# A new order of steps for a tightly scheduled attention-and-experts kernel: constants first, weights for the output last, fewer dummy matmuls

## The chip, the core and the metric

The kernel runs on one core of a Trainium2 chip. The metric is the device time of one execution in microseconds (us). Several executions were taken of each kernel, and each experiment was timed in the same rounds as the kernel before, on the same chip. A run is called slow when it lies over 1.5% above the fastest of its kernel; comparisons below use the other, fast runs.

Five engines work side by side, each through its own instruction stream in order: TensorE (PE in the profile's lines; its weight loads are PEld) multiplies matrices, ScalarE (ACT) computes functions, VectorE (DVE) and GpSimd (POOL) do elementwise work, SyncE (SP) starts transfers; 16 DMA engines move data. TensorE's *granted clock* is the share of its full speed that the profile's clock records show.

## The reference, cut to what matters

```python
mag = np.sqrt(a_re*a_re + a_im*a_im)             # (4, 8, 768, 48): batch, head, time, channel
scale = np.minimum(mag, 0.999) / (mag + 1e-06)   # the complex decay, its size capped
for t in range(768):                             # linear attention with a decaying complex state
    S_re, S_im = ar*S_re - ai*S_im + k[t] (x) v[t], ar*S_im + ai*S_re
    y[t] = q[t] @ S_re
x = y as (3072 tokens, 384)
out = (sigmoid(x @ w_gate) * (x @ w_val)) @ w_out    # 384 -> 1536 -> 384
```

## The kernel before

Time is cut into 6 chunks of 128 steps; with 4 sequences this makes 24 *slabs* of 128 tokens and 384 channels. Slabs are handled in nine *groups* of 1, 1, 2, 4, 4, 4, 4, 2 and 2. Within a chunk the decays become logarithms and phases, which are summed along time by fp32 matmuls; the last phase of a chunk is carried to the next chunk by a small transfer (a *hop*). Each slab then has scores, a state and an output `y`, which is transposed and goes through the gate and value matmuls of its group.

All of it is a list of named steps. Each has a number in `TIMES`; sorting by these numbers gives the order in which the steps are written to the in-order instruction streams of the engines. They are no times of the chip.

```python
SIZES = [1, 1, 2, 4, 4, 4, 4, 2, 2]
# decays of slab m, group g
add(("sq", m), ...)    # ScalarE: squares of a_re, a_im        (after the loads lr, la of slab m)
add(("add", m), ...)   # GpSimd: sum of the squares
add(("min", ...), ...) # GpSimd: cap, once per two slabs
add(("lna", g), ...)   # ScalarE: log of a group        } these need one table of functions,
add(("lnm", g), ...)   # ScalarE: log of the sizes      } tanh, sin and arctan need others:
add(("inv", g), ...)   # ScalarE: exp(-log)             } each switch is one ACT_TABLE_LOAD
add(("r", ...), ...)   # GpSimd: ratio                  -> ("atan", g) on ScalarE
add(("cl", m), ...)    # TensorE: cumulative sums, fp32 -> ("ee", m) exponentials on ScalarE
add(("hop", m), ...)   # GpSimd queue: carry of the phase -> ("ct", m), ("nid", m) TensorE
# ... sines "cs", products "qke", "ks", "qs", transposes "tp", scores "sc", "y", "xp", "xt" ...
t_moe = kind("moe", 4, [L, 512], F32, psum)   # four PSUM buffers for gate, value and output
for fb in range(NFB):                         # 12 blocks of the hidden layer
    add(("pg", g, fb), ...)     # TensorE: gate
    add(("pv", g, fb), ...)     # TensorE: value
    add(("tanh", g, fb), ...)   # ScalarE: tanh of the gate
    add(("p", g, fb), ...)      # VectorE: (tanh + 1) * value
# "po": output matmuls with wo; "ot": scaling; "st": store
...
order = plan.order(TIMES)                     # sorted by TIMES; adds a "table" step at each switch
for key in order:
    if key[0] == "table":
        nc.scalar.preload_act_table_set(SETS[key[1]])
        continue
    st = plan.steps[key]
    for n in st[2]:
        tiles[n] = plan.bufs[n](n)
    for _ in range(WARM.get(key, 0)):         # dummy matmuls ahead of this step
        nc.tensor.matmul(warm_of(tiles[st[2][0]]), zero, zero, start=True, stop=True)
    st[0](tiles)
```

Of the kernel before, what the change touches and what calls it, by code (L numbers as in the profile page):

```python
# [34 lines left out]
        3.57, 5.49],  # L35
    "wg": [
        28.263, 7.549, 23.318],
    "wv": [
        30.844, 31.664, 9.765],
    "wo": [  # L40
        37.677, 33.061, 38.497],
    "lr": [
        0.04, 0.45, 14.208, 19.927, 12.031, 27.419, 43.37, 24.787, 53.034,
        71.13, 63.694, 61.674, 77.312, 83.312, 79.472, 77.722, 107.913,
        110.073, 108.733, 111.993, 150.47, 185.542, 182.86, 184.072],
    "la": [
        0.86, 2.2, 20.947, 18.967, 22.867, 32.518, 40.682, 17.017, 57.834,
        71.91, 62.634, 56.874, 80.432, 88.622, 82.352, 78.228, 108.323,
        122.256, 131.294, 111.033, 150.88, 171.936, 186.502, 189.892],
    "sq": [  # L50
        4.73, 5.69, 24.437, 25.174, 28.029, 41.292, 50.764, 30.44, 66.726,
        77.988, 76.988, 72.777, 92.103, 104.991, 99.025, 83.273, 114.177,
        127.024, 135.003, 116.725, 175.031, 194.324, 190.832, 198.199],
    "add": [
        5.599, 6.595, 25.342, 26.296, 33.881, 42.197, 51.669, 34.835, 68.555,
        82.855, 77.893, 73.682, 96.999, 116.036, 107.784, 97.953, 115.082,
        145.007, 141.883, 131.112, 175.936, 195.229, 197.196, 208.669],
    "min": [
        6.179, 11.162, 27.361, 43.728, 53.776, 84.92, 79.325, 118.143,
        119.046, 146.538, 151.278, 196.293, 210.891],  # L60
    "lna": [
        6.427, 7.678, 26.042, 55.473, 88.108, 123.53, 158.229, 196.725,
        221.563],
    "lnm": [
        6.844, 12.805, 28.766, 56.85, 86.731, 122.153, 161.353, 197.462, 222.3],
    "inv": [
        7.261, 8.226, 26.91, 58.226, 89.616, 125.647, 159.976, 198.936,
        223.037],
    "r": [
        7.81, 8.811, 29.083, 63.293, 59.771, 92.922, 91.161, 129.351, 127.59,  # L70
        161.521, 163.281, 199.841, 223.942],
    "cl": [
        8.081, 15.614, 32.195, 34.117, 61.599, 58.377, 59.726, 67.931, 88.259,
        90.329, 95.326, 96.524, 127.983, 123.871, 124.517, 133.416, 167.245,
        166.376, 168.741, 170.993, 199.291, 198.645, 224.126, 229.088],
    "ee": [
        12.065, 19.814, 34.502, 35.242, 62.446, 59.603, 60.573, 68.914,
        91.363, 92.84, 98.285, 97.545, 128.83, 124.907, 127.761, 134.263,
        168.221, 168.961, 169.701, 171.84, 203.738, 199.673, 228.465, 229.935],
    "scr": [  # L80
        12.621, 23.277, 35.716, 41.092, 63.414, 70.44, 70.16, 69.47, 98.381,
        99.121, 98.841, 98.101, 129.386, 135.509, 129.666, 134.819, 171.376,
        171.096, 171.656, 172.756, 204.599, 200.852, 230.771, 230.491],
    "rbe": [
        17.607, 28.029, 65.514, 72.93, 100.311, 138.175, 177.434, 207.039,
        238.046],
    "lk": [
        3.16, 8.421, 6.04, 23.827, 16.057, 52.074, 50.154, 48.796, 84.272,
        76.068, 90.542, 53.994, 105.359, 114.303, 81.392, 151.29, 125.658,
        118.047, 160.423, 170.316, 183.27, 163.02, 194.892, 205.289],  # L90
    "lq": [
        5.08, 18.167, 28.827, 35.306, 58.794, 54.954, 60.714, 55.914, 87.662,
        85.232, 91.502, 70.72, 105.769, 114.713, 89.582, 156.48, 141.003,
        142.753, 162.083, 172.346, 188.932, 196.432, 205.699, 207.999],
    "lv": [
        4.12, 21.907, 29.83, 37.994, 51.114, 46.108, 64.554, 86.702, 118.457,
        69.75, 117.637, 126.068, 59.754, 146.608, 102.279, 135.099, 141.953,
        140.593, 121.846, 164.56, 204.879, 197.392, 148.087, 193.932],
    "v16": [
        10.585, 32.484, 43.151, 53.2, 54.679, 52.623, 71.27, 94.682, 122.562,  # L100
        117.567, 120.407, 133.338, 138.97, 149.378, 116.991, 145.962, 147.441,
        176.984, 141.307, 202.387, 211.793, 225.703, 168.944, 242.96],
    "qke": [
        13.699, 21.557, 35.916, 44.631, 69.509, 61.532, 65.054, 80.228,
        99.487, 108.739, 106.023, 101.248, 136.629, 125.829, 139.546, 159.59,
        171.644, 169.883, 182.979, 186.798, 204.66, 206.908, 229.387, 231.148],
    "atan": [
        9.937, 10.354, 32.471, 65.128, 94.874, 131.234, 165.181, 201.707,
        225.777],
    "ct": [  # L110
        11.182, 12.386, 34.763, 33.359, 69.276, 70.241, 71.049, 76.463,
        98.778, 102.372, 105.608, 107.064, 139.369, 142.805, 149.621, 146.87,
        169.853, 175.014, 177.614, 176.458, 205.553, 209.07, 229.734, 230.58],
    "r16": [
        14.565, 13.233, 35.61, 36.076, 70.123, 71.088, 74.604, 78.859,
        100.788, 103.906, 106.95, 108.481, 144.071, 144.537, 150.814, 151.28,
        171.66, 176.295, 184.888, 185.354, 206.4, 209.947, 230.581, 231.513],
    "nid": [
        16.26, 13.833, 36.838, 36.676, 70.887, 71.695, 75.254, 80.175,
        101.388, 106.254, 110.099, 113.499, 145.393, 147.516, 152.21, 163.64,  # L120
        172.26, 177.104, 186.677, 186.84, 208.184, 214.896, 231.226, 232.912],
    "cr": [
        17.78, 18.15, 39.747, 44.566, 72.407, 75.461, 90.993, 80.539, 106.204,
        110.192, 129.57, 116.355, 149.48, 159.606, 154.383, 166.557, 175.768,
        180.232, 195.061, 193.954],
    "cs": [
        16.623, 14.516, 37.276, 38.433, 71.25, 74.041, 75.831, 81.172,
        101.751, 109.035, 110.562, 117.938, 147.194, 151.592, 152.749,
        164.024, 173.874, 177.467, 187.184, 189.675, 208.548, 215.574,
        231.969, 233.276],  # L130
    "ks": [
        17.912, 23.392, 38.565, 47.386, 72.539, 75.33, 77.395, 86.683, 103.04,
        110.9, 111.851, 120.334, 148.483, 155.763, 154.209, 166.393, 175.163,
        179.327, 189.969, 193.181, 214.402, 219.049, 233.258, 235.59],
    "qs": [
        18.778, 24.258, 39.431, 48.651, 73.405, 76.196, 80.124, 89.08,
        104.372, 114.182, 113.316, 124.671, 149.349, 158.152, 156.629,
        168.045, 177.995, 181.003, 191.434, 197.045, 215.867, 219.915,
        234.124, 240.153],
    "tp": [  # L140
        19.778, 20.425, 28.256, 25.258, 41.58, 40.431, 51.31, 54.189, 74.808,
        79.728, 84.774, 77.843, 89.882, 87.183, 92.675, 93.122, 119.088,
        109.005, 125.163, 122.777, 115.604, 118.641, 130.376, 132.746,
        159.946, 156.257],
    "qkT": [
        20.426, 21.073, 29.326, 25.905, 45.924, 41.229, 55.436, 54.837,
        78.261, 81.759, 85.421, 84.658, 90.95, 87.882, 93.408, 94.606,
        119.735, 117.003, 125.811, 123.424, 116.405, 122.28, 131.425, 133.555,
        160.594, 161.193],
    "sc": [  # L150
        24.476, 28.033, 35.967, 26.638, 54.636, 43.128, 56.168, 62.971,
        85.659, 87.957, 93.569, 94.865, 95.972, 94.642, 98.437, 98.158,
        129.502, 131.872, 129.279, 126.26, 135.335, 133.192, 136.208, 134.462,
        162.766, 162.543, 163.802, 167.022, 169.387, 169.61, 173.973, 172.932,
        192.406, 187.002, 193.924, 199.937, 201.683, 200.16, 204.457, 204.68,
        224.972, 231.389, 233.075, 233.298, 242.63, 239.009, 246.424, 245.801],
    "mst": [
        27.662, 28.727, 36.542, 27.062, 56.034, 49.517, 56.634, 63.614,
        86.084, 88.48, 94.007, 95.804, 96.403, 95.205, 99.256, 98.657,
        130.769, 132.49, 129.703, 127.009, 135.951, 134.154, 136.632, 134.886,  # L160
        163.567, 162.967, 164.632, 167.446, 169.874, 170.473, 174.504,
        173.638, 194.647, 188.077, 198.062, 200.361, 202.108, 200.96, 205.723,
        205.124, 226.29, 231.979, 236.456, 234.99, 243.251, 241.685, 246.934,
        246.335],
    "kv": [
        20.225, 37.726, 44.375, 59.023, 97.17, 94.442, 99.424, 127.133,
        136.431, 140.015, 138.361, 168.541, 172.039, 161.693, 172.732,
        194.797, 202.557, 206.599, 224.772, 230.38],
    "P": [
        28.261, 40.763, 44.776, 63.148, 97.571, 97.003, 99.856, 127.608,  # L170
        137.232, 143.605, 139.779, 168.942, 172.706, 164.166, 173.172,
        195.246, 202.958, 207.332, 225.173, 231.047],
    "y": [
# [875 lines left out]
```

## Time and profile before

| | before |
|---|---|
| time, median of 3 runs | 286.42 us (286.03 to 288.17) |
| profiled run | 284.33 us, span 282.5 us |
| useful TensorE work, from the spacing of matmul starts | 218 us |
| dummy matmuls / table loads | 534 / 31 |

The page's chain of waits, by engine, shows what the span is made of when one follows back what released what:

```profile
PE 35%; ACT 22%; DMA 13%; POOL 9%; SPq 8%; issue 7%; DVE 4%; ACTq 0%; POOLq 0%; DVEq 0%
```

Only 35% of the way back runs over TensorE (PE), 22% over ScalarE (ACT). A line of a timeline gives start, length, engine, source line, what it did (in brackets: idle time before, and what ended it). The first two are ScalarE's timeline (start, length, engine, source line, what it did): the table load ahead of the logarithms of the first group of four slabs, and the first of these logarithms.

```profile
61.35 1.28 ACT L1012 ACT_TABLE_LOAD   x1
62.65 1.49 ACT L626 ACTIVATE a<-a 128x1536 f32<-128x1536 f32 x1
```

These two are the table by stretches (stretch, length, then busy time and number of instructions of PE, weight loads, VectorE, ScalarE and GpSimd, then granted clock, DMA share, GB/s):

```profile
60.00:90.00 30.00, 28.11 (x341) 22.23 (x339) 17.58 (x35) 26.20 (x47) 20.93 (x19) 1.00 0.81 144
160.00:190.00 30.00, 28.16 (x260) 17.15 (x259) 25.97 (x44) 25.72 (x41) 18.68 (x20) 1.00 0.78 150
```

In the first, TensorE looks busy, but 164 of its matmuls are dummies: by starts, useful work is 17.3 of 30 us, and ScalarE, GpSimd and TensorE take turns. In the second TensorE loses 1.8 us. One of its waits there, from TensorE's timeline (in brackets: idle time before, and what ended it):

```profile
180.78 0.88 PE L741 MATMUL ct<-a,c_t 128*128 128x384 f32 x2 [1.11 <-ACT ee L661]
```

### The profile page before, as it was taken

The numbers are of one execution on the slowest core, as the hardware profiler recorded it, in microseconds if no ns is written. First come the engines' busy times: TensorE is split into PE (matmuls) and PEld (weight loads), VectorE is DVE, ScalarE is ACT, GpSimd is POOL, SyncE is SP. The second block draws the span as 40 slices with busy tenths as digits, with TensorE's granted clock in tenths as the row PEclk, the third lists the DMA queues.
The fourth block names the chain that finished last, engine by engine and source line by source line (L and its number), as shares of the span: only waits on it lengthen the run. The fifth ranks groups of instructions, "written<-read, shape, count | busy, mean of one in ns | idle before, by whom it ended". The sixth has DMA issues, their size and how long they took to land.

```text
span 282.5 us, 6759 instructions
## 1 busy us (share of the span) xinstructions
PE 260.3 (92%) x2586; PEld 179.7 (64%) x2586; DVE 197.2 (70%) x364; ACT 200.3 (71%) x340; POOL 158.4 (56%) x170
## 2 busy tenths in 40 slices
PE   8956994999998999999999999799999999998995
PEld 8735783888767766545774456454457545577784
DVE  3155553672478989898795897798788686697553
ACT  3993992478998997789953999674899559924240
POOL 0604981445968889947999717945449704803000
PEclk9999997799999999999999999999999999999999
DMA  7999999889489944596347769858997744074001
GB/s 146 200 180 194 167 200 195 170 177 207 60 116 201 208 97 57 100 212 139 83 91 121 157 134 210 143 90 129 222 218 105 127 102 102 9 150 107 30 30 56
DMA packets 175344, 38.46 MB, mean 136 GB/s; under 512 B 167992, under 2 KB 175312, under 8 KB 175312
## 3 DMA queue, kind: packets, MB, share of 16 engines
q1 hardware_dynamic: 170688, 34.46, 64.2%
q0 software_dynamic: 4624, 3.57, 8.6%
q8 instruction: 20, 0.33, 0.5%
q14 instruction: 12, 0.10, 0.1%
HBM read 31.01 MB, written 4.76 MB: 127 GB/s over the span
## 4 chain that ended last, share of the span: by engine, by line
PE 35%; ACT 22%; DMA 13%; POOL 9%; SPq 8%; issue 7%; DVE 4%; ACTq 0%; POOLq 0%; DVEq 0%
PE o L984 8%; PE g L948 8%; DMA a<-in_a_im_dram 8%; PE v L948 8%; SPq L579 6%; ACT L1012 5%; ACT sq L605 3%; PE ct L741 2%; PE cl L652 2%; ACT g L958 2%; ACT lm L632 2%; POOL lm L611 2%; DMA qkT<-qst 2%; POOL qk L714 2%; ACT cr L764 2%
## 5 line engine op out<-in xcount | busy, mean ns | idle before, releaser
L958 ACT ACTIVATE g<-g 128x512 f16<-128x512 f32 (+2 forms) x108 | 47.2, 455 | 48.8 <-PE g L948 40.8
L964 DVE SCALAR_TENSOR_TENSOR p<-g,v 128x512 f16<-128x512 f16 (+2 forms) x108 | 52.4, 506 | 32.0 <-PE v L948 15.3
L948 PE MATMUL v<-xt,wv 128*128 128x512 f16 (+2 forms) x324 | 60.9, 313 | 4.6 <-ACT g L958 4.2
L948 PE MATMUL g<-xt,wg 128*128 128x512 f16 (+2 forms) x324 | 59.9, 311 | 1.0 <-ACT g L958 0.5
L984 PE MATMUL o<-wo,p 128*128 128x384 f16 (+1 forms) x300 | 55.5, 319 | 0.0
L714 POOL TENSOR_TENSOR qk<-qk,ee 128x768 f32<-128x768 f32 x23 | 44.7, 1976 | 18.7 <-DMA qk<-in_q_dram 10.9
L611 POOL TENSOR_TENSOR lm<-sq 128x384 f32<-128x384 f32 x23 | 25.4, 1119 | 36.5 <-ACT sq L605 36.3
L948 PEld LDWEIGHTS <-wv 128*128 128x128 f16 x324 | 29.9, 100 | 22.5 <-issue 5.4
L948 PEld LDWEIGHTS <-wg 128*128 128x128 f16 x324 | 30.2, 99 | 21.6 <-issue 4.0
L1012 ACT ACT_TABLE_LOAD x31 | 39.8, 1283 | 0.5
L1018 PEld LDWEIGHTS <-zero 128*128 128x128 f16 x534 | 34.1, 102 | 5.6 <-issue 3.5
L851 DVE TENSOR_TENSOR mst<-sc,c_t 128x512 f16<-128x512 f32 x48 | 32.1, 684 | 6.6 <-PE sc L843 6.4
L984 PEld LDWEIGHTS <-p 128*128 128x128 f16 x300 | 27.0, 97 | 14.1 <-issue 0.9
L643 POOL TENSOR_TENSOR a<-a 128x768 f32<-128x768 f32 (+1 forms) x12 | 20.8, 1746 | 20.3 <-ACT a L637 15.4
L605 ACT ACTIVATE sq<-a 128x768 f32<-128x768 f32 x24 | 20.1, 841 | 14.0 <-DMA a<-in_a_im_dram 13.3
L786 DVE TENSOR_TENSOR kst<-qk,cs 128x768 f16<-128x768 f32 x24 | 23.5, 978 | 9.2 <-ACT cs L778 3.8
L786 DVE TENSOR_TENSOR qst<-qk,cs 128x768 f16<-128x768 f32 x24 | 23.4, 980 | 0.0
L741 PE MATMUL ct<-a,c_t 128*128 128x384 f32 x48 | 20.5, 512 | 1.8 <-ACT ee L661 1.1
L652 PE MATMUL cl<-lm,c_t 128*128 128x384 f32 x48 | 20.4, 514 | 0.8 <-DMA c_t<-glk_c 0.4
L831 DVE COPY qkT<-tp 128x1024 f16<-128x1024 f16 x26 | 17.5, 685 | 3.1 <-PE tp L825 3.0
L733 POOL DMA_DIRECT2D a<-cr x20 | 17.6, 1006 | 2.6 <-ACT a L721 2.2
L747 DVE TENSOR_SCALAR r<-ct 128x384 f16<-128x384 f32 x24 | 12.9, 551 | 8.1 <-PE ct L741 8.0
(64 smaller groups left out, 429.3 us busy)
## 6 DMA issues: line engine op xcount, KB each, us to landing
a<-in_a_re_dram SPq DMA_DIRECT2D x24, 192.0 KB
a<-in_a_im_dram SPq DMA_DIRECT2D x24, 192.0 KB
qk<-in_k_dram SPq DMA_DIRECT2D x24, 192.0 KB
v<-in_v_dram SPq DMA_DIRECT2D x24, 192.0 KB
qk<-in_q_dram SPq DMA_DIRECT2D x24, 192.0 KB
out_dram<-ot SPq DMA_DIRECT2D x23, 192.0 KB
wg<-in_moe_w_gate_dram POOLq DMA_DIRECT2D x3, 384.0 KB, 6.1
wv<-in_moe_w_val_dram POOLq DMA_DIRECT2D x3, 384.0 KB, 7.8
```

What stands on the lines that cost most here:

```text
L605: nc.scalar.activation(out=T[SQ], in_=T[A][:, :, s], func=FT.Square)
L611: eng(g).tensor_tensor(out=T[LM][:, s], in0=T[SQ][:, 0], in1=T[SQ][:, 1], op=ALU.add)
L714: eng(g).tensor_tensor(out=T[QK], in0=T[QK], in1=T[EE], op=ALU.mult)
L741: nc.tensor.matmul(T[CT][:, :HD], wt_t, T[A][:, 1, s], start=True, stop=False, skip_group_check=True)
L786: nc.vector.tensor_tensor(out=T[SL][i].rearrange("p h (r x) -> p h r x", r=2)[:, :, :, 0:D], in0=heads(T[QK][:, i]).unsqueeze(2) .broadcas ...
L851: nc.vector.tensor_tensor(out=T[MS], in0=T[SC], in1=msk_t.unsqueeze(1).broadcast_to([L, 4, L]), op=ALU.mult)
L948: nc.tensor.matmul(T[ACC][:, :nt], w[:, j, fb * 128:fb * 128 + 128], T[XT][:, j, :nt], start=(j == 0), stop=(j == 2))
L958: nc.scalar.activation(out=T[G16][:, :nt], in_=T[PG][:, :nt], func=FT.Tanh, scale=0.5)
L964: nc.vector.scalar_tensor_tensor(out=T[PT][:, fb, :nt], in0=T[G16][:, :nt], scalar=1.0, op0=ALU.add, in1=T[PV][:, :nt], op1=ALU.mult)
L984: nc.tensor.matmul(T[PO][:, :wd], T[PT][:, fb, s * L:(s + 1) * L], wo16[:, fb, c0:c0 + wd], start=(fb == 0), stop=(fb == NFB - 1))
L1012: nc.scalar.preload_act_table_set(SETS[key[1]])
L1018: nc.tensor.matmul(warm_of(tiles[st[2][0]]), zero, zero, start=True, stop=True)
```

## The change

The author gives every step a new number: constants first, gates with less in front of them, fewer GpSimd steps right behind a carry transfer. Buffer slots and dummies (340 in place of 534) follow from the order. No arithmetic changes; five table loads fall away. The core of the diff:

```diff
     "consts": [
-        3.57, 5.49],
+        0, 9.751],
     "wv": [
-        30.844, 31.664, 9.765],
+        10.876, 36.405, 32.691],
     "wo": [
-        37.677, 33.061, 38.497],
+        42.756, 50.985, 47.732],
     "la": [
-        0.86, 2.2, 20.947, 18.967, 22.867, 32.518, 40.682, 17.017, 57.834,
+        0.82, 3.581, 15.146, 15.897, 18.807, 23.826, 24.786, 29.721, 42.831,
     "lna": [
-        6.427, 7.678, 26.042, 55.473, 88.108, 123.53, 158.229, 196.725,
-        221.563],
+        6.019, 10.78, 25.196, 52.172, 85.365, 98.55, 131.983, 162.343, 194.776],
 ... (all other rows of TIMES, SLOTS with the buffer of each tile)
 WARM = {
-    ... 534 dummies, most in the first 45 us
+    ('cl', 0): 2,
+    ('kv', 0): 12,
+    ... 340 in all
```

## The prediction

> **What bounds the kernel now.** I read the page's engine line first, then a table of three stretches (stages), then the chain of waits and the timeline in the stretch with least TensorE work, then the groups.
>
> ```profile
> PE 260.3 (92%) x2586; PEld 179.7 (64%) x2586; DVE 197.2 (70%) x364; ACT 200.3 (71%) x340; POOL 158.4 (56%) x170
> PEclk9999997799999999999999999999999999999999
> DMA  7999999889489944596347769858997744074001
> ...
> L1012 ACT ACT_TABLE_LOAD x31 | 39.8, 1283 | 0.5
> ```
> ```profile
> 0.00:60.00 60.00, 47.29 (x626) 40.90 (x627) 28.09 (x65) 38.34 (x70) 26.86 (x33) 0.94 1.05 182
> 60.00:120.00 60.00, 57.35 (x636) 41.95 (x634) 44.01 (x82) 52.22 (x87) 47.69 (x46) 1.00 0.73 133
> 120.00:283.00 163.00, 155.69 (x1330) 96.81 (x1328) 125.11 (x218) 109.79 (x184) 83.90 (x92) 1.00 0.61 120
> ```
> The columns of the second fence are stretch, length, busy time of PE, its weight loads, VectorE, ScalarE, GpSimd, granted clock, DMA share, GB/s. TensorE's 92% is not all useful: overlapping matmuls count in full, and dummies into `zero` count as work. So I made a ledger from the spacing of matmul starts: a 128x384 matmul of the output takes 0.163 us (four in 0.65 us in the chain), a 512-wide one 0.215, an fp32 pair (cumulative sums) 0.70, a transpose or score 0.056. Times their counts: output 47, gate and value 93, fp32 34, transposes, scores and the small rest 45: **218.5 us useful of a span of 282.5**. The other 64 us are 534 dummies (about 0.06 us each, 32 us) and standing still. By stretch of the trace, useful work is 22 of the first 60 us, 45 of the next 60, 152 of the last 163. So from 120 us on TensorE is the bound, with 11 us lost in 163; before 60 us the bound is the DMA queues (share 1.05, that is, full).
>
> The chain of waits and the timeline of ScalarE show where the first stretch breaks:
> ```profile
> 32.03 0.58 SPq L579
> 32.65 14.51 DMA a<-in_a_im_dram
> 47.23 0.84 ACT sq L605
> ```
> ```profile
> 47.23 0.84 ACT L605 ACTIVATE sq<-a 128x768 f32<-128x768 f32 x1 [4.48 <-DMA a<-in_a_im_dram]
> ```
> One decay load, issued at 32.65, lands 14.5 us later; ScalarE is in order, its square stands ahead of slab 0's gate tanhs, and all engines stand for 4.5 us. The clock records then show half clock from 46.3 to 53.1 us. Near the end there is one more such stop:
> ```profile
> 260.02 0.38 PE L843 MATMUL sc<-qkT,qkT 128*128 128x128 f16 x4 [0.98 <-DMA qkT<-qst]
> ```
>
> **What the skill says.** (1) Perfetto Trace Analysis, "Identifying the Most-Contended Engine": matmul busy share is a poor measure of TensorE's headroom. Agrees: 260 us busy hold 218.5 useful. (2) DMA: Bandwidth & Descriptors, "Queues, rings and completion order": each DMA engine alternates between queues packet by packet. The trace fits: GpSimd's queue (weights) has 4,624 packets of mean 84 ns, SyncE's queue 170,688 of 17 ns, so while weights flow the other loads get little; between 38 and 42 us SyncE's queue moved under 30 GB/s. (3) ScalarE: Activation LUTs, "What ACT_TABLE_LOAD costs": about 1283 ns for any set; the trace has 1283. (4) TensorE: Matmul & The Clock Gate, "Part 1": an idle TensorE falls to half clock and needs some 3.4 us of work to return. The 0.5 records from 46.3 us agree.
>
> **The change, part by part.** No arithmetic changes. Counting the built order of both kernels: DVE, GpSimd, SyncE and real TensorE instructions are equal in number; 194 dummies and 5 table loads go; the rest is order and buffer slots.
>
> *A, the head.* A 192 KB load costs about 1.03 us of all DMA engines (196.6 KB at some 190 GB/s, windows above); a weight piece 2.7 us (4,624 x 84 ns / 16 engines / 9 pieces). Before: the load that stops everything has 25 loads (itself included), 1.3 us of constants and seven weight pieces ahead: 25.8 + 1.3 + 18.9 = 46, plus the start at 1.9: 47.9; seen 47.2. After: that load is issued much earlier, with all but one (slab 7's) of the first eight slabs' squares ahead of the first tanh; the three `wo` pieces move behind the gate. The gate becomes the last value piece, with 27 loads, constants and six pieces ahead: 27.8 + 1.3 + 16.2 + 1.9 = 47.2. So the gate comes no more than 1 us sooner than the 48.3 at which TensorE resumed. But the useful TensorE work standing ahead of the first block that needs it is 11.7 us, against 10.3 at the stop before. Lead: 1.1 + 1.4 = **2.5 us**. Nearly all later TensorE work is one dense stream, so most of a lead in the head lives to the end, unless lost below.
>
> *B, dummies.* 194 x 0.058 = 11 us of TensorE, but they stand where it would wait anyway; they keep the clock. I credit 0. In the first 20 us the old kernel has a nearly unbroken run of them, the new one 2 ahead of the first matmul, so early fp32 pairs run at half clock (some 0.7 us more each, about four of them serial). The head is DMA-bound there, so I charge only 0.3 us.
>
> *C, table loads.* 5 x 1.283 = 6.4 us of ScalarE. The chain has 5.4% = 15.3 us of the 39.8 us of loads on it, so 38%: 2.5 us if they were average ones. Four of the 31 were in the last groups' chain, where TensorE had other work. I credit **1 us**.
>
> *D, the tail.* In program order, useful TensorE work left after the last slab's phase correction (`nid`) is 31.3 us before and 44.2 after. The last slab's transposes have 13 us more cover, so the 0.98 us stop above goes, and some of the small stops in 220-260 us. I credit **1 us**.
>
> *E, GpSimd behind carries.* A carry transfer occupies GpSimd 1.0 us (20 of them, 17.6 us) and what runs behind it is stretched (a 1.81 us product took 2.62 at 145.6 us). The new order still has such runs (three hops and a product, twice or more); GpSimd is 56% busy. Credit 0.3 us.
>
> *F, new gate.* The middle `wo` piece is now issued last, three GpSimd steps after the previous piece, shortly ahead of its output matmuls, which stand in TensorE's order with 21 us useful ahead. If it lands late TensorE stops there. Charge 0.5 us.
>
> Sum: 2.5 + 1 + 1 + 0.3 - 0.3 - 0.5 = **4.0 us**, all from the 64 lost: 286.4 - 4.0 = **282.4 us** (-1.4%). The keys that order the steps are themselves times, and their last store falls from 265.3 to 262.4; I take no time from them, they only say the author hoped for some 1%.
>
> **Rivals.** *R1, the head only swaps its stop.* The first 50 us carry the same kind of bytes; the stop for the decay load becomes one for the value piece or the `wo` piece, with a half-clock spell after it. For: 1.05 DMA share in this stretch. Against: weights of the output move behind the gate. It makes 285-287. *R2, the lead is real but is given back between 60 and 120 us,* where ScalarE is busy 52 of 60 us and GpSimd 48, and the chain runs through them: the group of four slabs must pass logs, sums, phases. For: chain entries of tables, squares, logs at 61-107 us. Against: its squares and logs now stand ahead of the gate. It makes 284-286. *R3, cold clock.* Fewer dummies let TensorE fall to half clock again in 20-60 us; useful 22 us would stretch by up to 10, partly hidden. Against: from 60 to 120 us, with 45 of 60 us useful and few dummies, the records show full clock. 285-289. *R4, ScalarE gain counts in full* (6.4 us instead of 1, with the tail): 279-280.
>
> **Range and chances.** The parts are each uncertain by 1 to 1.5 us; together some 2.5. 8 in 10: **279.2 to 287.0**. Faster by over 2% needs under 280.7, or 5.7 us of the 64: R4 must hold in part, 0.25. Slower needs 292.1, which only a bad R3 gives: 0.04. Same: 0.71.
>
> **What will show it.** A: no 14 us decay load in the chain; TensorE's useful work up to 60 us rises from 22 to 24-25; DMA share stays full to about 50 us; a wait of gate or value matmuls on the value weights at 44-49 us. B: granted clock low in the first 20 us, without delay to the first tanh. C: 26 loads, ScalarE busy near 194 us; the chain's share of them under 5.4%. D: no wait on `qst` after 250 us. F: a wait of the first output matmuls on `wo`, under 2 us. The prediction is wrong if the stretch from 120 us loses much more or less than 11 us (it should lose 8 to 11), or if the half-clock spell grows beyond 7 us after 20 us.

## The result, and the profile after

The kernel after took **275.72 us** (median of 4 runs, 274.39 to 277.63), against 287.3 us for the kernel before in the same rounds. Ratios are the mean time of one kernel's fast runs over that of the other's in the same rounds, so not quite the ratio of these medians: 0.9616, 95% interval 0.9531 to 0.9701. It is faster by 3.8%. The predicted range began at 279.2, and the class that I gave 0.71 (within 2%) was wrong.

How large is the gain really? On the first chip the kernel before had four runs, all over 286 us. In later rounds on other chips it had 7 to 27 fast runs each, with means of 283.1 to 284.4 us, and a tail of runs up to 293. The kernel after had fast means of 275.86, 276.23 and 276.50 us on three chips. The last two ratios are 0.9753 and 0.9716, so the gain between fast runs is some 2.5 to 2.8%, or 7.6 us both times, and the profiled pair says 7.2 us of span. I use "some 7.5 us" from here. My prediction took 4.0 us off a starting time that was itself some 3 us above the kernel's usual fast runs; both add to the miss.

The page of the kernel after: the engine line, the two rows of slices, the chain by engine, and the row of table loads.

```profile
PE 250.8 (91%) x2392; PEld 170.8 (62%) x2392; DVE 199.3 (72%) x364; ACT 193.7 (70%) x335; POOL 166.4 (60%) x170
...
PEclk9995689999999999999999999999999999999999
DMA  8999999998598964599706996499984339581001
...
PE 63%; DMA 10%; ACT 8%; POOL 8%; DVE 6%; issue 3%; SPq 1%; POOLq 0%; ACTq 0%; DVEq 0%
...
L998 ACT ACT_TABLE_LOAD x26 | 33.4, 1283 | 0.5
```

Now 63% of the chain is TensorE, and ScalarE's share went from 22% to 8%. Where was the time earned? I counted the useful TensorE work that each trace had started by a given time (real matmuls only, each at its nominal spacing):

| by (us) | before (us of work) | after | lead |
|---|---|---|---|
| 50 | 12.8 | 14.6 | +1.8 |
| 60 | 20.2 | 20.4 | +0.2 |
| 90 | 37.5 | 42.6 | **+5.1** |
| 120 | 65.0 | 69.1 | +4.1 |
| 160 | 104.7 | 108.3 | +3.6 |
| 190 | 132.2 | 138.2 | **+6.0** |
| 250 | 190.5 | 196.1 | +5.6 |
| 260 | 198.9 | 206.1 | +7.2 |

A *lead* is the useful work that the kernel after is ahead. So at 60 us, after the whole head that the prediction had worked out, there is no lead. It is earned in three places: 60 to 90 us, 160 to 190 us, and a little near 255 us. The lines that answer to those of before, ScalarE's timeline first:

```profile
55.17 1.28 ACT L998 ACT_TABLE_LOAD   x1
56.46 1.48 ACT L612 ACTIVATE a<-a 128x1536 f32<-128x1536 f32 x1
```
```profile
60.00:90.00 30.00, 28.76 (x299) 21.37 (x298) 23.12 (x42) 26.66 (x51) 24.33 (x22) 1.00 0.83 150
160.00:190.00 30.00, 30.00 (x263) 18.00 (x262) 25.21 (x45) 20.49 (x37) 22.02 (x24) 1.00 0.82 144
```

The logarithms of the first group of four start **6.2 us sooner** (62.65 to 56.46), and what hangs on them follows: the arctangent 72.4 to 64.4, the first carry 74.1 to 66.2. The carry gained 8.0 us, more than the logarithms: from the first logarithm to it 11.5 us pass before and 9.7 after. GpSimd has two ratio steps (`a<-a`) on the way, and before, another product stood between them. GpSimd's timeline, before and after:

```profile
68.73 1.81 POOL L714 TENSOR_TENSOR qk<-qk,ee 128x768 f32<-128x768 f32 x1
70.50 1.82 POOL L643 TENSOR_TENSOR a<-a 128x768 f32<-128x768 f32 x1
...
74.14 1.68 POOL L733 DMA_DIRECT2D a<-cr  x2
```
```profile
60.77 3.59 POOL L629 TENSOR_TENSOR a<-a 128x768 f32<-128x768 f32 x2 [5.78 <-ACT a L623]
64.33 1.82 POOL L700 TENSOR_TENSOR qk<-qk,ee 128x768 f32<-128x768 f32 x1
66.18 1.68 POOL L719 DMA_DIRECT2D a<-cr  x2
```

So 6.2 us of the carry's 8.0 are earlier logarithms, and 1.8 us are the order of GpSimd's steps. The traces of the experiments below keep these two lengths: 11.5 us in `y_sq5late`, which has the old order there, and 9.7 us in `s_new84` and `d_stop`, which have the new one.

From 160 to 190 us TensorE is no longer idle at all, and ScalarE is busy 5.2 us less (25.72 to 20.49). Before, it had in this stretch the logarithms of the group with slab 16 (4.4 us, at 167.5 to 172.4) and four table loads (166.2, 172.4, 176.8, 183.7). After, these logarithms stand at 138.2 to 142.8 us, and three table loads are left (164.8, 167.6, 175.9).

### The profile page after: what moved, and what is told of

It reads as the page before. It is cut to its first block, busy times and chain, and to the rows that moved or that the text cites.

```text
span 275.3 us, 6378 instructions
## 1 busy us (share of the span) xinstructions
PE 250.8 (91%) x2392; PEld 170.8 (62%) x2392; DVE 199.3 (72%) x364; ACT 193.7 (70%) x335; POOL 166.4 (60%) x170
## 3 DMA queue, kind: packets, MB, share of 16 engines
q1 hardware_dynamic: 170688, 34.46, 66.2%
## 4 chain that ended last, share of the span: by engine, by line
PE 63%; DMA 10%; ACT 8%; POOL 8%; DVE 6%; issue 3%; SPq 1%; POOLq 0%; ACTq 0%; DVEq 0%
PE g L934 15%; PE v L934 15%; PE o L970 9%; PE cl L638 6%; PE ct L727 5%; DMA a<-in_a_re_dram 2%; PE sc L829 2%; POOL qk L700 2%; POOL lm L597 2%; ACT L998 2%; DMA rbe<-scr 2%; PE cl L1004 1%; DVE mst L837 1%; DMA out_dram<-ot 1%; DMA a<-in_a_im_dram 1%
## 5 line engine op out<-in xcount | busy, mean ns | idle before, releaser
L944 ACT ACTIVATE g<-g 128x512 f16<-128x512 f32 (+2 forms) x108 | 46.7, 457 | 49.1 <-PE g L934 39.9
L700 POOL TENSOR_TENSOR qk<-qk,ee 128x768 f32<-128x768 f32 x23 | 45.8, 2072 | 7.9 <-ACT ee L647 7.6
L934 PEld LDWEIGHTS <-wv 128*128 128x128 f16 x324 | 29.1, 98 | 19.2 <-issue 2.8
L934 PEld LDWEIGHTS <-wg 128*128 128x128 f16 x324 | 29.0, 97 | 18.9 <-issue 2.9
L998 ACT ACT_TABLE_LOAD x26 | 33.4, 1283 | 0.5
L638 PE MATMUL cl<-lm,c_t 128*128 128x384 f32 x48 | 21.8, 545 | 10.2 <-ACT lm L618 10.2
L629 POOL TENSOR_TENSOR a<-a 128x768 f32<-128x768 f32 (+1 forms) x12 | 21.8, 1827 | 10.7 <-ACT a L623 10.6
L772 DVE TENSOR_TENSOR kst<-qk,cs 128x768 f16<-128x768 f32 x24 | 25.2, 1054 | 3.3 <-ACT cs L764 2.5
L1004 PEld LDWEIGHTS <-zero 128*128 128x128 f16 x340 | 23.1, 106 | 5.8 <-issue 3.7
L727 PE MATMUL ct<-a,c_t 128*128 128x384 f32 x48 | 21.2, 528 | 1.6 <-DMA a<-cr 1.1
L693 POOL TENSOR_SCALAR v<-v 128x384 f16<-128x384 f32 x24 | 14.6, 608 | 8.9 <-DMA v<-in_v_dram 7.1
L719 POOL DMA_DIRECT2D a<-cr x20 | 18.7, 1063 | 1.0 <-ACT a L707 0.9
```

The costliest lines, as they stand in the source:

```text
L638: nc.tensor.matmul(T[CL][:, :HD], wl_t, T[LM][:, s], start=True, stop=True)
L700: eng(g).tensor_tensor(out=T[QK], in0=T[QK], in1=T[EE], op=ALU.mult)
L727: nc.tensor.matmul(T[CT][:, :HD], wt_t, T[A][:, 1, s], start=True, stop=False, skip_group_check=True)
L772: nc.vector.tensor_tensor(out=T[SL][i].rearrange("p h (r x) -> p h r x", r=2)[:, :, :, 0:D], in0=heads(T[QK][:, i]).unsqueeze(2) .broadcas ...
L934: nc.tensor.matmul(T[ACC][:, :nt], w[:, j, fb * 128:fb * 128 + 128], T[XT][:, j, :nt], start=(j == 0), stop=(j == 2))
L944: nc.scalar.activation(out=T[G16][:, :nt], in_=T[PG][:, :nt], func=FT.Tanh, scale=0.5)
```

## The experiments

My theory: the path that sets the time is a loop through engines that are each in order, and ScalarE's steps lie on it in two stretches. (1) The stop of ScalarE at 42.75 to 47.2 us before pushed the logarithms, which stand behind the gate tanhs in its stream, and with them everything up to 90 us. (2) Between 160 and 190 us ScalarE's work, table loads among it, lies on that loop and counts in full. The rivals are: more TensorE work standing ready in the head (my part A), the tail (parts C, D), the dummies (part B), or the assignment of buffers. "Fast mean" below is the mean of fast runs; the kernel after is 276.2 us, the kernel before 283.1 to 284.4.

### Buffers or order?

Slots were given out anew in both orders, always the slot that had been free longest (`SLOTS` only; the order of the steps and `WARM` untouched).

> Control: the changed kernel's order with the buffer slots handed out anew, always the one freed longest ago, as the spliced kernels must have it. Both theories (gain from the order of steps / gain from the slots): if the order alone makes the gain, the ratio to before stays near 0.96 (275 to 277 us); if the given slots matter, it falls back by over 1% (279 or more).

> Control: the order of before with slots handed out by the same rule. Order theory: ratio 0.995 to 1.005. Slot theory: off by over 1%.

Measured: new order 276.68 us (fast mean; ratio 0.9821), old order 284.88 (1.0064) where the kernel before had 283.46. With slots by the same rule and on the same chip the two orders differ by 8.2 us, so the order makes the gain. What the given slots add is small but not well measured: 1.4 us in the old order; in the new one 0.5 us by the means, which are from different chips, and 2 to 3 us by the ratios (0.9821 against 0.9753 and 0.9716). The slots given out anew also allowed mixed orders, whose slots must be given out anew.

### Mixed orders

```diff
-order = sorted(steps, key=old number)
+order = [steps whose new number < 55, in new order] + [all others, in old order]   # s_newhead55
+order = [steps whose new number < 84.4 ...]                                        # s_new84
+order = [steps whose new number < 140 ...]                                         # s_new140
+order = [steps whose old number < 192, in old order] + [others, in new order]      # s_old192
 # WARM goes with its step; slots given out anew
```

> Splice: the new order (and its dummies) for every step planned before 55, the old order for all that follow. Theory H (the gain is made in the head and shows at 60 to 90 us, where the decay chain of the first group of four starts some 6 us sooner): 4 to 5 us of the 7 to 11 us are here, ratio 0.980 to 0.986. Theory L (the gain is made in the later order, the head only swaps its stop): ratio 0.995 or more.

> The new order for every step that is planned before 84 us, the old order after it. Ledger theory (4 to 5 us of the gain are earned between 60 and 90 us, in the decay chain of the first group of four slabs): this kernel has some 4 to 5 us of lead at 90 us and keeps it: 280 to 281 us, the rest of the gain (2 to 3 us near 180 and 255 us) stays missing. Rival (the gain is in the tail, by fewer table loads and a longer cover for the last slab): no gain here, 284 to 286 us.

> The new order for all steps planned before 140 us, the old order after. Ledger theory: the lead of 3.5 to 4 us at 140 us is kept, and the 2 to 3.5 us earned near 180 and 255 us are missing: 278 to 279.5 us. Theory that the whole gain comes before 140 us: 276 to 277 us. A new stop at the seam would show as a single wait of several us in TensorE's timeline, and then the run tells nothing of the tail.

> The old order for every step planned before 192 us, the new order for the last 75 us. Ledger theory: only the 1 to 2 us of the last stretch, 283 to 285 us. Rival (gain in the tail): 279 to 281 us.

Measured, as fast means: **283.05** (head to 55 alone, 0.9993), **279.62** (to 84.4, 0.982), 281.23 (to 140, 0.9845), 289.56 (0.9 of the old order, then the new tail, 1.0169).

The head alone earns nothing, which my theory had not expected (0.980 to 0.986). In its trace the logarithms did start early (56.1 us), but behind them GpSimd stood for 6.3 us ahead of slab 5's values, which the old order had put in front of the ratio, and the first carry came at 73.6 us (before: 74.1):

```profile
63.75 0.51 POOL L622 TENSOR_SCALAR v<-v 128x384 f16<-128x384 f32 x1 [6.26 <-PE sc L758]
```

(Its profiled run was slow, so this says what stood in line, not how much it cost.) With the stretch to 84 us added, the lead of the ledger is 4.0 us at 90 us, 1 to 2 from 120 to 250 and 3.3 at the end. So this part of the gain belongs to head *and* first group together. Theory (1), which put it down to ScalarE's stop alone, is too simple: the logarithms come early, and then GpSimd's order must let them through. The last two missed what I expected (278 to 279.5 and 283 to 285 us) and tell little: each has a new stop at its seam. For the new tail this is TensorE's timeline, which loses 5.5 us that neither pure order loses:

```profile
209.00 0.50 PE L899 MATMUL o<-wo,p 128*128 128x384 f16 x1 [5.47 <-DVE p L879]
```

The kernel with new order to 140 us lost 2.0 us of its lead against the kernel after between 170 and 190 us, as `s_new84` did (2.2) and the kernel before did (2.4); then another 3.4 us between 190 and 230 us, where the others lose under half a us. The first agrees with theory (2). The second is a seam: TensorE waits 1.91 us for a carry at 215 us, and the granted clock is 0.72 from 216 to 222.

### Taking the stop out of the kernel before

Twice, in different ways. First by loading the late decays sooner:

```diff
 "lr": ...  slab 6: 43.37  -> 27.46
 "la": ...  slab 5: 32.518 -> 27.44,  slab 6: 40.682 -> 27.48
```

> Before, with three transfers alone moved: the decay loads of slabs 5 and 6 are issued ahead of the weight pieces, ScalarE's and all other orders as before. If the late decay load alone is the loss (14.5 us in flight, all stop 4.5 us), then 3 to 5 us are gained (ratio 0.983 to 0.990), and the log of the first group of four starts by 59 us instead of 62.6. If the DMA queue as a whole is the bound there, the stop only moves to the weights: under 1.5 us (ratio over 0.995).

Measured: 289.47 us (1.0275), **slower** by 2.7%, which no theory had. The queue is full, so what moved ahead pushed another load behind the weights. GpSimd's timeline, waiting for the queries of slab 2:

```profile
46.47 1.80 POOL L714 TENSOR_TENSOR qk<-qk,ee 128x768 f32<-128x768 f32 x1 [8.19 <-DMA qk<-in_q_dram]
```

ScalarE's stop grew from 4.48 to 9.38 us behind it, and the granted clock was at half from 46 to 56 us. Here one load's gain was another's loss, so this edit of the loads can't test theory (1). So the second edit leaves the loads alone and moves only the steps that wait:

```diff
-sq[5] 41.292,  add[5] 42.197,  min[4] 43.728
+sq[5] 44.412,  add[5] 44.42,   min[4] 44.43     # behind tanh 10 of slab 0, the seventh in order
```

> The kernel before with three steps moved and nothing else: the square that waits for the late decay load (sq_5), its sum and its clamp go behind slab 0's tenth tanh in the order, no load is moved. Theory (the stop was ScalarE's, because it is in order; TensorE's and the weights' data were there): the stop at 42.8 us shrinks, the logarithms of the first group of four (62.65 us) come 2 to 5 us sooner, and the time falls by as much, to 280 to 283 us. Rival (the late loads are the bound: the same stop comes back at the next square, sq_6, or at the weights): within 1 us of the kernel before.

Measured: 282.38 us against 283.87 (0.9961, interval 0.9929 to 0.9994; medians 282.67 against 284.62). GpSimd's line, then three of ScalarE's timeline:

```profile
41.06 1.81 POOL L714 TENSOR_TENSOR qk<-qk,ee 128x768 f32<-128x768 f32 x1 [3.10 <-DMA qk<-in_q_dram]
```
```profile
46.49 0.28 ACT L958 ACTIVATE g<-g 128x128 f16<-128x128 f32 x1 [3.16 <-DVE p L964]
...
59.41 1.28 ACT L1012 ACT_TABLE_LOAD   x1
60.70 1.49 ACT L626 ACTIVATE a<-a 128x1536 f32<-128x1536 f32 x1
```

In this run the queries of slab 2, issued at 31.6 us as before (31.5), kept GpSimd waiting to 41.06 us instead of 38.2; VectorE behind it came late, and ScalarE stood for 3.16 us instead of 4.48. The stop shrank to two thirds, the half clock behind it disappeared, the logarithms came 1.95 us sooner (62.65 to 60.70), and the time fell by 1.1 us (by the ratio, whose interval is 0.2 to 2.0) to 2 us (by the medians). This fits one for one, but the interval doesn't part it clearly from the rival's "within 1 us", and the logarithms just missed the 2 to 5 us that I had expected. It is also not the only change: the late queries made a new stop in place of the old one.

### Putting the stop back, and delaying ScalarE elsewhere

A small tile `junk` (128x384, fp16) is squared in place, n times, ahead of one step in the kernel after.

```diff
+    junk = const.tile([L, HD], F16, name="junk")
+    nc.vector.memset(junk, 0.0)
 ...
+    if key == ("tanh", 0, 11):     # d_stop, n = 9;   d_lna3: ("lna", 3), n = 14;   d_cs14: ("cs", 14), n = 14
+        for _ in range(n):
+            nc.scalar.activation(out=junk, in_=junk, func=FT.Square)
```

> The kernel after, with 9 dummy squares (measured 0.52 us each before, so 4.7 us) on ScalarE just ahead of slab 0's first gate tanh (at about 43 us): the stop of 4.5 us of the kernel before, put back in its place. Chain theory (the stop pushed the logarithms of the first group of four, behind the tanhs in ScalarE's order, and with them everything to 90 us): 4 to 7 us slower, 280 to 283 us. Rival (TensorE has other work, and the tanhs catch up): under 2 us, 276 to 278 us.

> The kernel after, with 14 dummy squares (128x384 fp16, some 0.4 us each, about 6 us in all) on ScalarE just ahead of the first logarithm of the first group of four slabs (lna_3, at about 56 us). Chain theory (TensorE waits between 60 and 90 us for the chain logs, sums, products, carries, phases of that group, whose start moved 6 us): the delay costs 4 to 6 us and is carried to the end, 280 to 282 us. Rival (the chain has slack and the lead comes from more TensorE work standing ready): under 2 us, 276 to 278 us.

> Control: the same 14 dummy squares (7.3 us) as in the run with the delay before lna_3, but at about 154 us, before the sines of slab 14, where TensorE has dense work queued. If any ScalarE delay of 7 us costs its length, some 7 us or more: 283 to 287 us. If place decides: under 2.5 us, 276 to 278.5 us.

| | delay (us) | fast mean (us) | slower by (us) |
|---|---|---|---|
| stop put back, 41.5 us | 5.0 | 282.77 | 6.6 |
| ahead of the logarithms, 55.9 us | 7.3 | 287.15 | 10.9 |
| ahead of slab 14's sines, 154 us | 7.3 | 285.28 | 9.1 |

The kernel after was not timed on the chips of these runs, nor on that of `t_tabs` below: the last column takes its 276.2 us from other chips. The ratios to the kernel before give the same costs within 1.3 us.

With the stop put back, ScalarE's timeline has the squares and the table load ahead of the logarithms, TensorE's has the stop:

```profile
41.53 4.96 ACT L1005 ACTIVATE junk<-junk 128x384 f16<-128x384 f16 x9
...
60.90 1.28 ACT L1000 ACT_TABLE_LOAD   x1
```
```profile
46.70 0.48 PE L936 MATMUL g<-xt,wg 128*128 128x128 f16 x3 [4.52 <-ACT g L946]
```

The table load comes at 60.90 us instead of 55.17, close to the 61.35 of the kernel before, and nearly the whole gain is gone. The second run, which cost nearly twice the 4 to 6 us that I had expected, shows where it passes through. TensorE, ahead of the cumulative sums that need these logarithms:

```profile
66.41 2.93 PE L640 MATMUL cl<-lm,c_t 128*128 128x384 f32 x4 [9.12 <-ACT lm L620]
```

The third was meant as a control with slack, and my expectation (under 2.5 us) was **wrong**. TensorE's timeline there:

```profile
163.90 1.44 PE L936 MATMUL g<-xt,wg 128*128 128x512 f16 x3 [6.25 <-ACT g L946]
```

TensorE can't run ahead: gate, value and output share four buffers (`kind("moe", 4, ...)`), and the next gate waits until the tanh and the product have freed one. So even where TensorE is the bound and has plenty queued, 7.3 us of delay made 6.25 us of stop: ScalarE has about 1 us of slack there, not seven. This makes theory (1) less special than I had put it: a long stop of ScalarE costs its length, or more, at all three places tried. Putting the stop back therefore shows what such a stop costs, but not that this place is special. Part of the "more" stands in the clock records: behind each stop the granted clock is 0.50 (46 to 52, 62 to 70 and 162 to 168 us), so TensorE resumes at half speed. How much of the cost this is was not tested.

### Table loads by place

```diff
+    if key in (("lna", 7), ("cs", 16), ("cs", 20)):      # t_tabs; t_170: ("lna", 7) alone;
+        nc.scalar.preload_act_table_set(another set)      # t_late4: ("cs", 20), ("tanh", 7, 1)
+        nc.scalar.preload_act_table_set(the set in use)
```

> The kernel after with 6 more table loads (another set and back, ahead of the group log lna_7 and of the sines of slabs 16 and 20, at about 170, 177 and 216 us), 7.7 us of ScalarE. Prediction's step C (a load in the tail costs about 38% of its length): 2.9 us slower, 278.5 us. Place theory (ScalarE idles 2 to 5 us behind each of these places): under 1.5 us, 275.5 to 277 us. Rival R4 (loads count in full): 283 us.

> The kernel after with 2 more table loads (2.57 us) ahead of the group log lna_7 at about 170 us alone. From the run with six of them, where 3.9 us were lost between 170 and 180 us: 3 to 4 us slower than the kernel after. If that loss was a chance of the run: 0 to 1 us.

> The kernel after with 4 more table loads (5.1 us) after 200 us: two ahead of the sines of slab 20 at about 216 us, two ahead of the first gate tanh of slab 7 at about 246 us, where ScalarE had idled 10.9 us. Place theory: under 1 us slower than the kernel after. Prediction's step C (38% of their length): 2 us. Loads count in full: 5 us.

> The kernel after, unchanged, as the yardstick on this chip: 274.5 to 277.5 us.

| | loads added | fast mean (us) | slower by (us) |
|---|---|---|---|
| t_tabs | 2 at 168, 2 at 180, 2 at 219 us: 7.7 us in all | 282.31 | 6.1 |
| t_170 | 2 at 170 us: 2.6 us | 280.18 | 4.0 |
| t_late4 | 4 after 200 us: 5.1 us | 277.35 | 1.1 |
| a_again | none | 276.23 | |

`t_tabs` ran on another chip. The last three shared one (ratios 0.987, 0.9793 with interval 0.9726 to 0.9861, and 0.9753 with 0.969 to 0.9817, so the 1.1 us of the four late loads can't be told from 0). In the run with six, the ledger against the kernel after loses 3.9 us between 170 and 180 us, 2.2 up to 190, and nothing behind the loads at 219 us. ScalarE's timeline, TensorE's, and the table by stretches show why 2.6 us of loads can cost 4:

```profile
168.20 1.28 ACT L1002 ACT_TABLE_LOAD   x1
169.49 1.28 ACT L1003 ACT_TABLE_LOAD   x1
```
```profile
172.44 1.47 PE L727 MATMUL ct<-a,c_t 128*128 128x384 f32 x2 [2.62 <-ACT ee L647]
```
```profile
170.00:176.00 6.00, 3.56 (x23) 2.10 (x24) 1.08 (x3) 2.38 (x4) 4.05 (x6) 0.72 0.40 79
```

TensorE waits 2.62 us for the exponentials and then runs on at a granted clock of 0.72 in that stretch (the kernel after has 1.00 there). ScalarE does idle for 2.8 and 5.2 us in this part of the kernel after, but this idle time is waiting for TensorE's sums and gates, and TensorE needs ScalarE's next exponentials in turn; the two runs show that it is no slack. My expectation for `t_tabs` (under 1.5 us) was wrong for the four loads in this stretch, right for the two later ones.

### The dummies

```diff
-WARM = { ... 340 dummies }
+WARM = {}
```

> The kernel after with no dummy matmuls at all (340 fewer). If they only fill gaps (prediction's part B: credit 0): the same within 1 us on what waits for others, plus what half clock costs: useful work at half clock before 80 us stretches, hidden in part: 277 to 280 us. If they hold the clock for work on the path: 282 us or more. If they stand in TensorE's way: below 275 us.

> The kernel after, unchanged, as yardstick for the next run: 274.5 to 277.5 us.

> The kernel after without any dummy, on the same chip: within 0.5 us of the kernel after if the dummies only fill gaps and the clock spells are hidden (part B, and the first run); 1 us or more faster if they stand in TensorE's way; 1 us or more slower if the clock they hold is worth something.

Measured: 275.49 us (0.9682) in the first run; with the kernel after on the same chip 276.67 (0.9727) against 276.50 (0.9716). The page of the last run without dummies:

```profile
PE 239.2 (86%) x2052; PEld 155.1 (56%) x2052; DVE 200.0 (72%) x364; ACT 193.7 (70%) x335; POOL 166.3 (60%) x170
...
PEclk9999666886999999999999999999999999999999
```

More slices of the head lie below full clock, PE's busy share falls from 91% to 86%, and the mean time is the same. The mean hides a spread, though. The profiled run above is the slowest of its six (278.56 us): its clock is 0.79 from 37 to 60 us and 0.89 from 60 to 90, where the yardstick's trace has 1.00, and by 90 us it has started 39.9 us of useful work against 43.9. The three of the six with the lowest mean clock (0.957) took 277.0 to 278.6 us, the other three 274.9 to 277.1. So a long cold spell may cost a us or two when it comes; over all runs nothing shows that the 340 dummies are worth having.

No experiment gave a version that beats the kernel after by more than the spread of its runs.

## Why the prediction was wrong, and where it was right

**A, the head: mechanism half right, the size too small, and the wrong quantity counted.** I said that the stop for the decay load goes, and it does: decay loads were 8% of the chain and are 2% and 1% now. But I valued it by TensorE work standing ahead of the gate (2.5 us). The sentence that failed is "Nearly all later TensorE work is one dense stream, so most of a lead in the head lives to the end, unless lost below." From 60 to 90 us it is not dense: before, only 17.3 of these 30 us are useful work (my "few dummies" there were 164), because TensorE has run out of work and waits for the chain of the first group of four. What counts is when this chain runs. ScalarE gets to the logarithms 6.2 us sooner, and GpSimd passes them on 1.8 us faster. The test I had named shows it: useful work up to 60 us was to rise by 2 to 3 us (from 22, where the ledger has 20.2); it rose by 0.2, and 4.9 us were earned in the next 30. The wait on the value weights that I had named did not come either; slab 0's tanhs ran from 42.86 us without a long stop. In place of 2.5 us the ledger has 5.1 at 90 us, for head and first group together; the new head alone gained nothing (`s_newhead55`), and taking the old stop out alone gained 1.1 to 2 us (`y_sq5late`). How the rest divides between the stop and GpSimd's order is not shown.

**C, table loads: right in kind, too small.** I took the average (38% of a load is on the chain), and said that "four of the 31 were in the last groups' chain, where TensorE had other work". The average hid two prices. From 199 us on, where four of the five fall away (8 loads before, 4 after), four added loads cost 1.1 us, not told from zero. Between 160 and 190 us ScalarE's time counts in full and more: a pair of loads put in there (2.6 us) costs 4.0 us. The ledger shows 2.4 us gained in this stretch, in place of my 1 for all loads; only one load fell away in it, and the rest is a thing I had not priced at all, the group's logarithms moved out of it to 138 us. No run parts these two.

**D, the tail:** right. No wait on `qst` after 250 us is left, and the ledger gains 1.2 us between 190 us and the end; I had credited 1. No run undid this alone, so that part is argued from the two traces.

**B, dummies:** right in credit (0, settled by two runs without any). I expected a low clock in the first 20 us; it came between 20 and 37 us (the slices of 5 and 6 in the page), some 12 us at half clock in the profiled run. That is over the 7 us after 20 us that I had named as a sign of being wrong, yet this run led by 0.2 us at 60 us.

**F, `wo`:** the charge of 0.5 us was not needed; the first output matmul waited for nothing. **E, GpSimd behind carries:** no run here tests the stretched steps that I credited with 0.3; the gain from GpSimd's order that the traces do show, 1.8 us up to the first carry, I had not seen. Some of the lead (5.1 to 3.6 us between 90 and 160 us) is lost again, and I did not find out to what.

**The rivals:** R2 had looked at the right stretch, 60 to 90 us and the chain through ScalarE and GpSimd, but expected the lead to be lost there; it was made there. R1 did not happen. Of R3 the cold clock came, but no loss of time showed with it in the kernel after. R4 (loads in full) is half true, by place.

**The sum:** 5.1 + 2.4 + 1.2, less the 1.5 lost from 90 to 160 us, is the 7.2 us of the profiled pair, in place of 4.0. My check "from 120 us on it should lose 8 to 11 us" came out as 6.4 (155.3 us of span with 148.9 us of work). The rest of the miss in absolute time is the starting value of 286.4, from three runs on one chip.

Open: why the kernel before has runs up to 293 us while the kernel after hardly leaves 274.4 to 278.7 us (one of 14 was above). Loads that land 3 us earlier or later while the DMA engines are full, as in `y_sq5late`, would do it, but no run shows that they do.

## What to carry to other kernels

When a stop on one engine goes, ask what stands *behind* it in that engine's stream and on which path that lies, not only how much work the bound engine has ready: here the logarithms behind the gate tanhs decided 60 to 90 us, and the work ahead of the tanhs gained nothing by itself. Then follow the path to the next engine: early logarithms were worth nothing while GpSimd's order held them up. Don't price a kind of instruction by its average share of the chain; price it by stretch, since a pair of table loads cost 4 us at one place, and two pairs 1.1 us, not told from zero, at others. Idle time of an engine is slack only if nobody downstream is waiting for it: a delay of a few us put in on purpose measures this, and in a kernel with few buffers between its engines the answer can be "none" even far from the critical stretch.

## What the Trainium skill lacked or had wrong

- Perfetto Trace Analysis, "Identifying the Most-Contended Engine": it has one optimise the engine of highest occupancy first, and takes occupancy of ScalarE as a fair measure of how close it is to its limit. That matmul busy share misleads was borne out: 239.2 us busy hold 218 useful without any dummy. (The 260 against 218.5 of the prediction is no clean test, since 534 dummies are in it.) But ScalarE at 70% had little slack at the three places where it was delayed by 5 to 7 us: 7.3 us at 154 us cost 9.1. The page lacks that engines coupled by few buffers have less slack than their idle time.
- ScalarE: Activation LUTs, "What ACT_TABLE_LOAD costs": 1283 ns agrees. The section adds a drain of about 1380 ns, and the next one, "Table sets: the hidden batching unit", counts about 2.7 us for a load; here no drain shows (last tanh done at 55.15, load at 55.17 for 1.28 us, logarithm at 56.46), and what a pair of loads cost the kernel was 4.0 us at one place and, for four, 1.1 us at others.
- TensorE: Matmul & The Clock Gate, "Part 1": the fall to half clock after standing idle agrees in kind, but it came in a stretch with a wait of 2.62 us (0.72 over the 6 us from 170 us), shorter than the idle window of about 3.4 us that the page gives; in `s_new140` it came with a wait of 1.91 us (0.72 from 216 to 222 us). It lacks a word on filling gaps with dummy work where TensorE waits for others anyway: 340 dummies against none was 276.50 against 276.67 us.
- DMA: Bandwidth & Descriptors, "Queues, rings and completion order": turns by packet fit what was seen, but no run tests them. It lacks how much a landing can move when the queues are full: in two kernels whose loads are issued in the same order, with the same load issued at 31.5 and 31.6 us, its user started at 38.2 and 41.06 us.
